# A list scheduler's table of costs and ranks: shorter ways for transfers, a steeper rank for the preparation of later pairs, a lower one for splitting the second weights

## The chip, the core and the metric

The kernel runs on one core of a Trainium2 chip. Its engines are TensorE (PE; its weight loads are listed as PEld), VectorE (DVE), ScalarE (ACT), GpSimd (POOL) and SyncE (SP), which issues nearly all transfers. The metric is device time in microseconds (us), lower is better, given as a median of several runs. One further run was recorded by the profiler; its rows are what is read below.

## The reference, cut to what matters

Three layers follow one another. The first is a recurrence over 768 time steps, for 4 x 8 heads with a 40 x 40 state each:

```python
for t in range(S):                      # S = 768
    y[:, :, t] = einsum('bhd,bhde->bhe', rt, state)
    Sa = einsum('bhde,bhe->bhd', state, at)
    state = state * wt[:, :, None, :] - einsum('bhd,bhe->bhde', Sa, bt)
    state = state + einsum('bhd,bhe->bhde', vt, kt)
x = y.transpose(0, 2, 1, 3).reshape(3072, 320)
x = maximum(maximum(x @ w1, x @ w2), x @ w3) @ w_out      # 320 -> 768 -> 320
x = ((x @ w_a) * (x @ w_b)) @ w_out2                      # 320 -> 1536 -> 320
```

The weights arrive as 64-bit numbers and are split in the kernel into a high and a low part.

## The kernel before, in words

The 768 steps are cut into 24 chunks of 32 steps, and two chunks make a pair (12 pairs, numbered 0 to 11). Inside a chunk the recurrence becomes a small triangular system, so that most of it is matrix work.

**Preparation of a pair** (`prep`, lines 355 to 487, and `solve`, 489 to 544) does not need the state. It loads the pair's inputs, forms running products of the decay (L395, L399 on VectorE), multiplies (L403, L413, L415), forms the products of keys (L446 or L428 on TensorE, L453 or L434 on VectorE), and sends them through DRAM to another layout (L460 writes BD, L466 reads BU). `solve` inverts the triangular blocks by many small steps: a product (L500 on GpSimd, or L501 on VectorE, as the scheduler picks) and a sum (L502 on VectorE). Its results go through DRAM again by two routes: TXp to TD (L472) to TT (L476), and TC to ED (L481) to NB (L484).

**The chain** (`chain`, from line 547) carries the state from chunk to chunk: L617 (it needs ZL), L631 (it needs TT), L644 (it needs NB), L664 (the new state), with copies on ScalarE and sums on VectorE (L672) between them, and at the side the output: L690, L702, L720. The first chunk of a pair is the first to need that pair's TT and NB. A pair's output goes through DRAM (L733 to L740) to the second layer.

**The second layer** (`moe_a`, L828 and L853 to L857 on TensorE) takes 192 matmuls for each pair, and can begin once the pair's output is there and its weights are split (`weights_a`, L760 to L785). **The third layer** (`moe_b`, L982, L990 to L992) begins when all chunks are done; its own weights are split before that by `stage_b` (18 pieces: L920 loads one, L750 to L753 and L922 to L924 split it, L927 and L928 write it to DRAM as WD), and `weights_b` (L934 to L938) fetches them from there.

**What sets the order.** Nothing of this order is written by hand. Each operation is given to a list scheduler (`Plan`) with an engine (or several to choose from), a duration, its reads and writes and a rank `pri`, where a lower one goes first. Ahead of the run the rank is lowered by 0.04 for each microsecond of the longest way from the operation to the end. The scheduler then walks through a modelled time and places whatever can start first; within 0.05 us the better rank wins. Each engine executes in the order so found, and SP issues its transfers in that order too: an instruction that waits holds up all behind it on its engine. A transfer is modelled as 1.2 us from the readiness of its inputs to its issue (`pre`), 0.4 us or more of SP, and a way `lat` until it has landed. The scheduler also inserts fillers (L276: a 128 x 128 matmul of a constant into a free bank, of no use to the result) where its model of TensorE's clock shows too little work.

Of the kernel before, what the change touches and what calls it, by code (L numbers as in the profile page):

```python
# [28 lines left out]
DMIN = 0.4  # L29
# [19 lines left out]
class Plan:  # L49
# [8 lines left out]
    def op(self, eng, dur, fn, r=(), w=(), ps=(), fin=(), pri=0.0, lat=None, after=(), pre=0.0, cls=0, alt=(), act=1.0, bias=None):  # L58

        i = len(self.ops)  # L60
        deps = set(after)
        for k in r:
            if k in self.lw:
                deps.add(self.lw[k])
        for k in w:
            if k in self.lw:
                deps.add(self.lw[k])
            deps.update(self.rd.get(k, ()))
        for k in r:
            self.rd.setdefault(k, []).append(i)  # L70
        for k in w:
            self.lw[k] = i
            self.rd[k] = []
        deps.discard(i)
        ways = {eng: (dur, fn, 0.0)}
        ways.update({e: (d, f, bias if bias is not None else 0.0 if pri < BIASP else BIAS) for e, d, f in alt})
        self.ops.append(dict(i=i, ways=ways, bias=bias, deps=deps, ps=tuple(ps), fin=tuple(fin), pri=pri, lat=lat, pre=pre, cls=cls, act=act))
        return i
# [159 lines left out]
def body(nc, tc, ia, out_ap):  # L238
    from contextlib import ExitStack

    V, A, G, T, SP = nc.vector, nc.scalar, nc.gpsimd, nc.tensor, nc.sync
    es = ExitStack()
    P = Plan(8)
    op = P.op
    npair = NP

    def dv(n, ps=False):
        return 0.15 + n * 0.00105 if ps else 0.12 + n * 0.0014

    def ac(n):  # L250
        return 0.17 + n * 0.0009
# [2 lines left out]
        return 0.4 + n * 0.0023  # L254

    def dma(fn, nbytes, r=(), w=(), pri=0.0, pre=1.2):
        return op("SP", max(DMIN, nbytes / 300e3), fn, r=r, w=w, pri=pri, lat=2.0 + nbytes / 200e3, pre=pre)

    def adma(fn, nbytes, r=(), w=(), pri=0.0, after=()):

# [93 lines left out]

    def prep(p):
        b, kb_ = p % NPB, p % 2
        pr = -0.5 + 0.6 * p
        P_, K_, Z_ = Pp[b], KT[kb_], ZL[b]
        parts = [(0, 1), (1, 2)] if p < NSPL else [(0, 2)]

# [23 lines left out]
        for cc in range(2):  # L384
# [8 lines left out]
            else:  # L393
# [8 lines left out]
               r=[("R", cc, 0), ("R", cc, 1), "d1"], w=rc, pri=pr)  # L402
# [4 lines left out]
            for src, k, n in ((Rp[:, cc, :, 0:32], rc, 1), (P_[:, cc, :, 1:33], pc, 0)):  # L407
                op("ACT", 0.61, lambda w_, cc=cc, src=src, n=n: A.activation(
                    Rp[:, cc, :, 0:32], src, AF.Square, accum_out=gd[:, 4 * p + 2 * cc + n:4 * p + 2 * cc + n + 1]),
                   r=k, w=rc + ["gd"], pri=pr + 0.5)  # L410
            for g in range(2):
# [3 lines left out]
                   r=pc, w=[("Za", b, g, cc)], pri=pr, alt=[("DVE", dv(512), lambda w_, cc=cc, g=g, r0=r0: V.tensor_tensor(  # L415
                       Z_[r0:r0 + 64, cc, g], Z_[r0:r0 + 64, cc, g], P_[r0:r0 + 64, cc, :, 0:32], ALU.mult))])
            pn = ("a", "kb", p, cc)
            za = [("Za", b, g, cc) for g in range(2)]
            if p >= KG:
# [12 lines left out]
                for n in range(4):  # L432
# [5 lines left out]
                       r=[pn, "con"], w=[("Zk", b, g, cc)], fin=[pn] if n == 3 else (), pri=pr)  # L438
# [12 lines left out]
            for g in range(2 if p < KG else 0):  # L451
# [4 lines left out]
                   r=[pn, "con"], w=[("Zk", b, g, cc)], fin=[pn] if g else (), pri=pr)  # L456
# [30 lines left out]
                16e3, r=[("ED", b, h) for h in range(2)], w=[("NB", p % 2, j)], pri=pr)  # L487

    def solve(p):
        pr = -0.5 + 0.6 * p  # L490
        cnt = [0]

        def mm(out_v, tmpshape, a, bb, rk, wk):
            i = cnt[0] % 2
            cnt[0] += 1
            n = int(np.prod(tmpshape))
            names = "abcd"[:len(tmpshape)]
            kw = {k: v for k, v in zip(names[1:], tmpshape[1:])}
            tv = TP[i][:, 0:n].rearrange("p (" + " ".join(names) + ") -> p " + " ".join(names), **kw)
            op("POOL", 0.35 + n * 0.0026, lambda w_: G.tensor_tensor(tv, a, bb, ALU.mult), r=rk, w=[("TP", i)], pri=pr,  # L500
               alt=[("DVE", dv(n), lambda w_: V.tensor_tensor(tv, a, bb, ALU.mult))])  # L501
            op("DVE", dv(n, True), lambda w_: V.tensor_reduce(out_v, tv, AX.X, ALU.add), r=[("TP", i)], w=wk, pri=pr)  # L502

        def diag(tile, off, blk, cnt_, rows, cols, rs=32, cs=1):
            base = tile[:, 0:1, 0:1]
            a = base.copy() if False else base
            return bass.AP(tensor=a.tensor, offset=a.offset + off, ap=[list(a.ap[0]), [blk, cnt_], [rs, rows], [cs, cols]])

        bu = [("BU", 0), ("BU", 1)]
        for t in range(1, 8):  # L510
            a = diag(TX, 0, 264, 2, t, t)
            u = diag(BU, t, 264, 2, 1, t, 0, 32)
            u = bass.AP(tensor=u.tensor, offset=u.offset, ap=[list(u.ap[0]), [264, 2], [0, t], [32, t]])
            o = diag(TX, t, 264, 2, t, 1)
            o = bass.AP(tensor=o.tensor, offset=o.offset, ap=[list(o.ap[0]), [264, 2], [32, t]])
            mm(o, (2, t, t), a, u, bu + ["TX"], ["TX"])

        def prod(dst, d_off, d_rs, L, l_off, l_rs, R, r_off, r_rs, nr, nt, nj, rk, wk):
            tl = 512 // (nt * nj)
            for c0 in range(0, nr, tl):  # L520
                k = min(tl, nr - c0)
                lb, rb, db = L[:, 0:1, 0:1], R[:, 0:1, 0:1], dst[:, 0:1, 0:1]
                a = bass.AP(tensor=lb.tensor, offset=lb.offset + l_off + c0 * l_rs, ap=[list(lb.ap[0]), [l_rs, k], [0, nt], [1, nj]])
                u = bass.AP(tensor=rb.tensor, offset=rb.offset + r_off, ap=[list(rb.ap[0]), [0, k], [1, nt], [r_rs, nj]])
                o = bass.AP(tensor=db.tensor, offset=db.offset + d_off + c0 * d_rs, ap=[list(db.ap[0]), [d_rs, k], [1, nt]])
                mm(o, (k, nt, nj), a, u, rk, wk)


        prod(TW, 0, 8, TX, 0, 32, BU, 8, 32, 8, 8, 8, bu + ["TX"], ["TW"])
        prod(TX, 8, 32, TW, 0, 8, TX, 264, 32, 8, 8, 8, ["TX", "TW"], ["TX"])  # L530

        op("ACT", 0.3, lambda w_: A.activation(BU[64:128, 0:8, 16:32], BU[0:64, 8:16, 16:32], AF.Copy), r=bu, w=[("BB", 0)], pri=pr)
        for h in range(2):
            op("ACT", 0.35, lambda w_, h=h: A.activation(TU[64 * h:64 * h + 64], TX[64:128, :, 0:16], AF.Copy), r=["TX"], w=[("TU", h)], pri=pr)
        k = bu + [("BB", 0), ("TU", 0), ("TU", 1)]
        prod(TC, 0, 16, BU, 16, 32, TU, 0, 16, 8, 8, 8, k, ["TC"])
        prod(TC, 8, 16, BU, 16, 32, TU, 8, 16, 8, 8, 16, k, ["TC"])
# [208 lines left out]
    def convert(raw, ca, m, kr, ka, pri, w=()):  # L746

        hi, lo = (lambda: raw()[:, :, 1]), (lambda: raw()[:, :, 0])
        a = lambda: ca()[:, 0:m]
        op("DVE", 0.12 + m * 0.0012, lambda w_: V.tensor_scalar(a().bitcast(U32), hi(), 3, 0x3FFFFFFF, ALU.logical_shift_left, ALU.bitwise_and), r=[kr], w=[ka, *w], pri=pri)  # L750
        op("DVE", dv(m), lambda w_: V.scalar_tensor_tensor(hi(), hi(), 0xC0000000, a().bitcast(U32), ALU.bitwise_and, ALU.bitwise_or), r=[ka], w=[kr], pri=pri)
        op("DVE", 0.12 + m * 0.0012, lambda w_: V.tensor_scalar(a().bitcast(U32), hi(), 0xFF800000, None, ALU.bitwise_and), r=[kr], w=[ka], pri=pri)
        op("DVE", dv(m), lambda w_: V.scalar_tensor_tensor(lo().bitcast(F32), lo(), 2.0 ** -52, a(), ALU.mult, ALU.mult), r=[ka], w=[kr], pri=pri)  # L753
# [157 lines left out]
    def stage_b():  # L911

        wk, ck = [("wraw", 0), ("wraw", 1)], [("wca", 0), ("wca", 1)]
        r = wrw[:, 0:960].bitcast(U32).rearrange("p (m k) -> p m k", k=2)
        h, a = wrw[:, 960:1440], wcw[:, 0:480]
        for ff in range(LV):
            for q in range(2):
                pr = 3.0
                cs = slice(480 * q, 480 * q + 480)
                dma(lambda w_, ff=ff, cs=cs: SP.dma_start(r, ia["wpb"][ff][:, cs].bitcast(U32).rearrange("p (m k) -> p m k", k=2)), 492e3, w=wk + ["sr", "sw"], pri=pr)  # L920
                convert(lambda: r, lambda: a, 480, "sr", "sa", pr, w=ck)
                i = op("ACT", ac(480), lambda w_: A.activation(h.bitcast(F32R), r[:, :, 1].bitcast(F32), AF.Copy), r=["sr"], w=["sh"], pri=pr)  # L922
                sub = lambda E: (lambda w_: E.tensor_tensor(a, r[:, :, 1].bitcast(F32), h, ALU.subtract))
                add = lambda E: (lambda w_: E.tensor_tensor(a.bitcast(F32R), a, r[:, :, 0].bitcast(F32), ALU.add))  # L924
                op("POOL", po(480), sub(G), r=["sr", "sh"], w=["sa"], pri=pr, alt=[("DVE", dv(480), sub(V))])
                op("POOL", po(480), add(G), r=["sr"], w=["sa"], pri=pr, alt=[("DVE", dv(480), add(V))])
                op("ACT", 0.3, lambda w_, ff=ff, cs=cs: A.dma_start(WD[ff, 0, :, cs], h), r=["sh"], w=[("WD", ff, q, 0), "sw"], pri=pr, lat=3.0, after=[i])  # L927
                dma(lambda w_, ff=ff, cs=cs: SP.dma_start(WD[ff, 1, :, cs], a), 246e3, r=["sa"], w=[("WD", ff, q, 1)] + ck, pri=pr)  # L928
# [334 lines left out]
```

## Time and profile before

| | us |
|---|---|
| runs (median of 3) | 1087.15, 1092.65, 1097.81 (1092.65) |
| the profiled execution's own time | 1090.93 |
| its span, from first to last instruction | 1088.7 |
| first matmul of the third layer (L982) | at 689.4 |
| last output product of the chain (L720) | at 640.38 |

The span falls into a start (0 to 140 us, with hardly any second layer yet), a middle (140 to 640, chain, preparation and second layer interleaved), the rest of the second layer (640 to 690), and the third layer (690 to the end). In the rows below, a matmul of float32 data such as L276 or L617 leaves two records for each instruction, so that a count of 494 stands for 247 instructions; a float32r matmul (L828, L982) leaves one. A busy time counts pipelined matmuls with their whole length; the distance between the starts of two of them is what they cost in time.

### The profile page before, as it was taken

How to read it: one execution, taken by the hardware profiler on the slowest of the kernel's cores; microseconds unless marked ns; L12 is line 12 of the kernel's file. 1: busy time of each engine (PE TensorE's matmuls, PEld its weight loads, DVE VectorE, ACT ScalarE, POOL GpSimd, SP SyncE). 2: the span in 40 equal slices, each digit the busy share in tenths (PEclk: the TensorE clock that was granted, in tenths of full speed). 3: DMA queues.
4: the chain of work that ended last, by engine and by line, in shares of the span. 5: the costliest groups of instructions: out<-in, count | busy, mean ns of one | idle time of the engine just before them, and what ended most of it. 6: DMA issues, size and time to landing. Idle time of an engine off the chain costs nothing.

```text
span 1088.7 us, 34319 instructions
## 1 busy us (share of the span) xinstructions
PE 1034.9 (95%) x14868; PEld 936.6 (86%) x14868; DVE 654.0 (60%) x1091; ACT 480.7 (44%) x1115; POOL 230.1 (21%) x198
## 2 busy tenths in 40 slices
PE   8999789999899998999899999999999999999997
PEld 7878778988798888898889899988888888888886
DVE  7896698968797875989587633475223232332222
ACT  6246546555647373847375532343222232222221
POOL 4441365533423222323320200011000000000000
PEclk9998899899999989999899999999999999999999
DMA  8846875656666847577655547742002000000000
GB/s 272 199 96 161 173 158 126 157 140 167 158 167 153 190 117 189 136 168 166 150 135 149 136 122 204 200 104 62 10 1 54 1 25 1 2 25 1 25 1 27
DMA packets 173437, 123.10 MB, mean 113 GB/s; under 512 B 122464, under 2 KB 147168, under 8 KB 172320
## 3 DMA queue, kind: packets, MB, share of 16 engines
q1 hardware_dynamic: 170688, 116.41, 43.4%
q10 hardware_dynamic: 2592, 4.42, 1.2%
q8 instruction: 119, 1.95, 0.8%
q14 instruction: 38, 0.31, 0.1%
HBM read 93.07 MB, written 27.72 MB: 111 GB/s over the span
## 4 chain that ended last, share of the span: by engine, by line
PE 70%; DVE 12%; DMA 8%; issue 4%; SPq 3%; ACT 1%; POOL 1%; DVEq 0%; POOLq 0%; ACTq 0%
PE bank L982 24%; PE bank L828 11%; PE bank L992 4%; PE bank L990 4%; PE bank L991 4%; PE bank L276 3%; DMA NB<-ED 2%; PE bank L664 2%; PE bank L720 2%; PE bank L644 2%; PE bank L702 2%; PE bank L853 2%; PE bank L854 1%; PE bank L617 1%; PE bank L855 1%
## 5 line engine op out<-in xcount | busy, mean ns | idle before, releaser
L1000 DVE TENSOR_TENSOR bas<-bank,bas 128x512 f32<-128x512 f32 x72 | 49.7, 691 | 188.8 <-PE bank L982 179.8
L982 PE MATMUL bank<-bxhi,bw 128*128 128x512 f32 x576 | 156.3, 393 | 0.0
L982 PEld LDWEIGHTS bank<-bxhi,bw 128*128 128x128 f32 x576 | 106.2, 188 | 20.8
L999 ACT ACTIVATE bas<-bank 128x512 f32<-128x512 f32 x72 | 43.0, 598 | 148.2 <-PE bank L982 144.2
L1002 ACT ACTIVATE bgh<-bas 128x512 fp32r<-128x512 f32 x72 | 45.5, 633 | 125.5 <-DVE bas L1000 125.5
L828 PE MATMUL bank<-xhi,whi 128*128 128x256 f32 x432 | 95.5, 303 | 0.0
L843 DVE TENSOR_TENSOR hm<-bank,hm 128x512 f32<-128x512 f32 x72 | 49.5, 688 | 67.0 <-PE bank L828 66.1
L982 PE MATMUL bank<-bxlo,bw 128*128 128x512 f32 x288 | 89.8, 393 | 0.0
L992 PE MATMUL bank<-bo,bgl 128*128 128x320 f32 x288 | 89.0, 309 | 0.4 <-DVE bgl L1003 0.4
L990 PE MATMUL bank<-bo,bgh 128*128 128x320 f32 x288 | 89.0, 309 | 0.0
L991 PE MATMUL bank<-bo,bgh 128*128 128x320 f32 x288 | 88.9, 309 | 0.0
L828 PE MATMUL bank<-xlo,whi 128*128 128x256 f32 x432 | 88.5, 287 | 0.0
L828 PE MATMUL bank<-xhi,wlo 128*128 128x256 f32 x432 | 88.2, 286 | 0.0
L413 POOL TENSOR_TENSOR ZL<-ZL,Pp 64x512 f32<-64x512 f32 x44 | 58.7, 1334 | 85.4 <-DVE Pp L395 75.0
L1003 DVE TENSOR_TENSOR bgl<-bas,bgh 128x512 fp32r<-128x512 f32 x72 | 49.8, 691 | 43.0 <-ACT bgh L1002 42.8
L276 PE MATMUL bank<-con 128*128 128x128 f32 x494 | 69.2, 293 | 4.0 <-DMA con<-in_con_dram 2.8
L828 PEld LDWEIGHTS bank<-xhi,whi 128*128 128x128 f32 x432 | 67.6, 194 | 2.6
L276 PEld LDWEIGHTS bank<-con 128*128 128x128 f32 x494 | 62.9, 203 | 7.6 <-ACT bank L344 2.8
L828 PEld LDWEIGHTS bank<-xlo,whi 128*128 128x128 f32 x432 | 68.6, 195 | 0.0
L828 PEld LDWEIGHTS bank<-xhi,wlo 128*128 128x128 f32 x432 | 68.4, 195 | 0.0
L982 PEld LDWEIGHTS bank<-bxlo,bw 128*128 128x128 f32 x288 | 54.1, 188 | 12.2
L828 PE MATMUL bank<-xt,wt 128*128 128x256 f32 x216 | 62.0, 287 | 0.0
(181 smaller groups left out, 2446.0 us busy)
## 6 DMA issues: line engine op xcount, KB each, us to landing
wraw<-in_wpb_dram SPq DMA_DIRECT2D x18, 480.0 KB
KT<-in_kb_dram SPq DMA_DIRECT2D x20, 384.0 KB
Pp<-in_wf_dram SPq DMA_DIRECT2D x10, 528.0 KB
Rp<-in_wr_dram SPq DMA_DIRECT2D x10, 528.0 KB
wraw<-in_wpa_dram SPq DMA_DIRECT2D x12, 384.0 KB
bw<-WD SPq DMA_DIRECT2D x9, 512.0 KB
WD<-wraw ACTq DMA_DIRECT2D x18, 240.0 KB
WD<-wca SPq DMA_DIRECT2D x18, 240.0 KB
```

The lines of the kernel that those rows point to most:

```text
L276: P.keep = lambda b: T.matmul(bank[b][:, 0:128], ident, ident, start=True, stop=True)
L413: op("POOL", po(512), lambda w_, cc=cc, g=g, r0=r0: G.tensor_tensor(Z_[r0:r0 + 64, cc, g], Z_[r0:r0 + 64, cc, g], P_[r0:r0 + 64, cc, :, 0: ...
L828: T.matmul(ps, w, x, start=(i == 0), stop=(i == 7))
L843: op("DVE", dv(512, True), lambda w_, pn=pn: V.tensor_tensor(f(hm), bank[w_[pn]], f(hm), ALU.max), r=[pn], w=["hm"], fin=[pn], pri=ep)
L982: T.matmul(ps, w, x, start=(k == 0), stop=(k == 7))
L990: T.matmul(o, gh[:, c], oh, start=ff == 0, stop=False)
L991: T.matmul(o, gh[:, c], ol, start=False, stop=False)
L992: T.matmul(o, gl[:, c], oh, start=False, stop=ff == 11)
L999: op("ACT", ac(512), lambda w_, j=j, pa=pa: A.activation(tb["as", j], bank[w_[pa]], AF.Copy), r=[pa], w=[("bas", j)], fin=[pa], pri=ep)
L1000: op("DVE", dv(512, True), lambda w_, j=j, pb=pb: V.tensor_tensor(tb["as", j], bank[w_[pb]], tb["as", j], ALU.mult), r=[pb], w=[("bas", j) ...
L1002: op("ACT", ac(512), lambda w_, j=j, k=k: A.activation(tb["gh", k], tb["as", j], AF.Copy), r=[("bas", j)], w=[("gh", k)], pri=ep)
L1003: op("DVE", dv(512), lambda w_, j=j, k=k: V.tensor_tensor(tb["gl", k], tb["as", j], tb["gh", k], ALU.subtract), r=[("bas", j), ("gh", k)], ...
```

## The change

Three numbers of the scheduler's tables change, and no operation is added or removed. The way of a transfer issued by SP becomes 1.4 us plus 4 us per MB in place of 2.0 plus 5. The rank of `prep(p)` and `solve(p)`, which was -0.5 + 0.6 p, becomes -0.5 + p. The rank of `stage_b`, which was 3, becomes 4.

```diff
     def dma(fn, nbytes, r=(), w=(), pri=0.0, pre=1.2):
-        return op("SP", max(DMIN, nbytes / 300e3), fn, r=r, w=w, pri=pri, lat=2.0 + nbytes / 200e3, pre=pre)
+        return op("SP", max(DMIN, nbytes / 300e3), fn, r=r, w=w, pri=pri, lat=1.4 + nbytes / 250e3, pre=pre)
...
     def prep(p):
...
-        pr = -0.5 + 0.6 * p
+        pr = 1.0 + p - 1.5
...
     def solve(p):
-        pr = -0.5 + 0.6 * p
+        pr = 1.0 + p - 1.5
...
-                pr = 3.0
+                pr = 4.0
```

As nearly every transfer is counted shorter, the longest ways and with them all ranks move too, and the order of every engine comes out differently.

TensorE, around L631 of chunk 4 (the first chunk of pair 2; TT_141 is its TT). Before:

```order
L446 MATMUL bank_64<-ZL_126,KT_125 64x32 x32
L276 MATMUL bank_67<-con 128x128 x11
L631 MATMUL bank_67<-Zs,TT_141 32x40 x32
L276 MATMUL bank_63<-con 128x128 x9
L446 MATMUL bank_63<-ZL_126,KT_125 64x32 x32
L828 MATMUL bank_68<-xhi,whi 128x256 x2
```

Now:

```order
L276 MATMUL bank_67<-con 128x128 x6
L631 MATMUL bank_67<-Zs,TT_141 32x40 x32
L828 MATMUL bank_68<-xhi,whi 128x256 x2
L828 MATMUL bank_68<-xhi,wlo 128x256 x2
L828 MATMUL bank_68<-xlo,whi 128x256 x2
```

Twenty fillers around this product have become six, the key products of a later pair (L446) have moved away from it, and second-layer matmuls follow it at once.

SP, between the write of TC (L481) and the read of NB (L484) of pair 3 (ED_77 and NB_145). Before:

```order
L476 DMA TT_139<-TD_74 32x16x32 x4
L738 DMA xf<-XD_80 128x2x256
L481 DMA ED_77<-TC 64x128 x2
L863 DMA X2D_83<-x2s 128x512
L460 DMA BD_72<-ZL_127 32x16x32 x2
L740 DMA xf<-XD_80 64x256 x2
L460 DMA BD_72<-ZL_127 32x16x32
L375 DMA Rp<-in_wr_dram 128x1056
L484 DMA NB_145<-ED_77 16x16x16 x4
```

Now:

```order
L476 DMA TT_139<-TD_74 32x16x32 x4
L466 DMA BU<-BD_72 64x512
L466 DMA BU<-BD_72 64x496
L481 DMA ED_77<-TC 64x128 x2
L484 DMA NB_145<-ED_77 16x16x16 x4
L928 DMA WD<-wca 128x480
L920 DMA wraw<-in_wpb_dram 128x960
```

Seven issues stood between the write and the read, and now none does; the next pair's BU reads, which came later, stand ahead of both.

## Rows read from the trace of the kernel before

**Rows 1.** The page's head: span, busy time and share of each engine.
```profile
span 1088.7 us, 34319 instructions
PE 1034.9 (95%) x14868; PEld 936.6 (86%) x14868; DVE 654.0 (60%) x1091; ACT 480.7 (44%) x1115; POOL 230.1 (21%) x198
```

**Rows 2.** Windows by stage: length, busy of each engine, PEclk, DMA share, GB/s.
```profile
0.00:140.00 140.00, 126.66 (x2383) 109.95 (x2384) 107.46 (x194) 72.93 (x191) 53.90 (x50) 0.95 0.72 178
140.00:640.00 500.00, 466.02 (x10007) 434.59 (x10007) 395.40 (x657) 288.41 (x718) 168.56 (x142) 0.96 0.63 152
640.00:690.00 50.00, 50.00 (x469) 49.58 (x469) 16.82 (x28) 11.45 (x21) 0.73 (x1) 1.00 0.75 210
690.00:1089.00 399.00, 392.18 (x2015) 342.49 (x2013) 134.31 (x214) 107.87 (x187) 6.87 (x6) 0.99 0.11 30
```

**Rows 3.** Group of the fillers: busy us, mean ns, idle before.
```profile
L276 PE MATMUL bank<-con 128*128 128x128 f32 x494 | 69.2, 293 | 4.0 <-DMA con<-in_con_dram 2.8 <-DVE XY L724 1.1
```

**Rows 4.** Timeline of PE, 482 to 484: start, length, work; then around 640.
```profile
482.24 0.28 PE L856 MATMUL bank<-hhi,woh 128*128 128x256 f32 x1
482.36 0.28 PE L857 MATMUL bank<-hlo,woh 128*128 128x256 f32 x1
482.48 1.50 PE L276 MATMUL bank<-con 128*128 128x128 f32 x12
483.74 0.48 PE L828 MATMUL bank<-xhi,whi 128*128 128x256 f32 x2
...
640.38 1.42 PE L720 MATMUL bank<-YL,YR 128*40 128x32 f32 x64
```

**Rows 5.** Waits of the span: engine, line, releaser; us, times, longest.
```profile
PE bank L644 <- DMA NB<-ED: 13.6, 9, 3.2
PEld bank L631 <- DMA TT<-TD: 6.9, 10, 2.3
PEld bank L644 <- DMA NB<-ED: 6.7, 6, 2.5
PE bank L631 <- DMA TT<-TD: 5.9, 11, 2.2
```

**Rows 6.** Timeline of SP, 209 to 220: start, length of issue.
```profile
209.31 3.58 SPq L481 DMA_DIRECT2D ED<-TC  x2
...
218.57 1.91 SPq L484 DMA_DIRECT2D NB<-ED  x4
```

**Rows 7.** Chain of waits around 220 and 376: start, us, what; one issue of NB and its landing.
```profile
220.03 3.14 DMA NB<-ED
376.86 4.63 DMA NB<-ED
```

**Rows 8.** One tile, NB: issue durations min/median/max ns, first and last start.
```profile
L484 SPq DMA_DIRECT2D NB<-ED x48: 303/446/628, 63.6 to 616.4; - x48
```

**Rows 9.** Groups of VectorE by form: busy us, mean ns.
```profile
L843 DVE TENSOR_TENSOR hm<-bank,hm 128x512 f32<-128x512 f32 x72 | 49.5, 688 | 67.0 <-PE bank L828 66.1 <-ACT hm L841 0.2
L399 DVE TENSOR_TENSOR_SCAN Rp<-Rp,d 128x528 f32<-128x528 f32 x24 | 35.0, 1458 | 0.5 <-DMA Rp<-in_wr_dram 0.3
L395 DVE TENSOR_TENSOR_SCAN Pp<-Pp,d 128x528 f32<-128x528 f32 x24 | 30.2, 1256 | 3.7 <-DMA TXp<-in_eye_dram 1.9 <-DMA Pp<-in_wf_dram 1.7
```

**Rows 10.** Windows of 20 us: length, busy PE, PEld, DVE, ACT, POOL, PEclk, DMA, GB/s.
```profile
360.00:380.00 20.00, 18.49 (x205) 17.75 (x203) 16.53 (x25) 5.24 (x10) 6.58 (x6) 1.00 0.81 197
380.00:400.00 20.00, 18.38 (x512) 16.63 (x514) 12.75 (x29) 12.56 (x32) 7.68 (x8) 0.83 0.37 83
```

**Rows 11.** One tile, BU: products of solve, durations min/median/max ns.
```profile
L501 DVE TENSOR_TENSOR TP<-BU,TU x19: 1014/1041/2099, 53.4 to 564.4; 128x512 f32<-128x512 f32 x19
L500 POOL TENSOR_TENSOR TP<-BU,TU x17: 1524/1693/3561, 52.6 to 604.4; 128x512 f32<-128x512 f32 x17
```

**Rows 12.** One tile, bw: first transfer's issue and the first L982.
```profile
L982 PE MATMUL bank<-bxhi,bw x576: 387/394/398, 689.4 to 1075.9; 128*128 128x512 f32 x192
L934 SPq DMA_DIRECT2D bw<-WD x9: 366/594/604, 648.2 to 682.2; - x9
```

## The prediction

> **What bounds the kernel now.** First read the head and the windows by stage [rows 1, 2]. TensorE is busy 95% of the span, and the four stages differ. From 690 us on it is never without work for long, nothing else is near its limit, and those 399 us hold only work that the change leaves as it is. From 640 to 690 it is busy throughout with what is left of the second layer. So whatever the change does, it does before 640, where TensorE is busy 593 of 640 us and VectorE 503 of 640. There, read who waits for whom [rows 5]: TensorE waits at L644 for NB and at L631 for TT. These are the two products by which a pair's preparation enters the chain. TensorE's two parts together stand still 20.3 us for NB and 12.8 us for TT. The chain itself is not what is short: between the first products of a pair and its L644 stand second-layer matmuls and fillers, and it is the preparation, VectorE's and GpSimd's many small steps and four transfers in a row, that comes last.
>
> Then the fillers [rows 3]. 494 records are 247 instructions. In the timeline [rows 4] six of them (12 records) occupy TensorE from 482.48 to 483.74, so one costs 0.21 us at the full clock, and all of them some 52 us. Together with the waits and the stretches at half clock (below) this is TensorE's time that holds no useful work, and only this can change.
>
> **The change part by part.** No operation appears or goes. What moves is read from the two orders, what it costs from the rows.
>
> *Fillers.* The order now has 217 of them, 30 fewer: 30 x 0.21 = 6.3 us less. Before L617 of chunk 5 there are 170 in place of 211, and at that place 152 second-layer matmuls have been done in place of 96. So the saving early in the kernel is real work in a filler's place and not an empty place only. Later some comes back: from chunk 12 to 19 the new order adds 27 fillers, the old one 12, since with the second layer further ahead nothing of it is ready (at L644 of chunk 12 exactly 960 matmuls, all five pairs that can be, are done). Bounds: 6.3 us of gain where nothing waits instead, 0 where the data come no earlier and each filler's time becomes a wait. I take the gain, because the useful matmuls that moved in show that the place is not empty.
>
> *Shorter ways.* For NB (16 KB) the scheduler now counts 1.46 us in place of 2.08, for ED 1.53 in place of 2.16, for BD, BU, TD and TT some 1.92 in place of 2.65. With `pre` and the issue this makes for NB 3.06 us from ready to landed, and it was 3.68. The trace has 3.14 us from one issue to the landing, and 4.63 in a busier place [rows 7]. So the new number is a little under the lower row, the old one between the two. What follows is two things of opposite sign.
>
> First, TensorE's instructions may be placed too early. ED and NB follow each other, so the plan can ask for NB 0.62 + 0.63 = 1.25 us sooner in each of the pairs 2 to 11: 12.5 us of waits at most. How much of that the order shows: I added up VectorE's work between the last sum of `solve` (L502 into TC) and the second L672 of the chunk that needs it, by the means of VectorE's groups (the costliest are in [rows 9]). Over pairs 3 to 11 it is 123 us before and 120 now, so the cover of the two transfers shrinks by 0.3 us a pair only. I take 3 us of loss.
>
> Second, SP issues closer. Between the write of TC (L481) and the read of NB (L484) 67 other issues stood in the 12 pairs, now 40. In pair 3 they cost much: ED was issued from 209.31 to 212.89, and NB only at 218.57 [rows 6], though a way of 3.14 us would have ended by about 216. At the median of 0.446 us [rows 8], 27 fewer issues are 12 us of SP's time. But SP must now wait for ED at the head of its queue, with the second weights' transfers and the next chunk's loads behind it, so the most is not to be had. Bounds 0 to 12 us of gain. I take 0, as only the pairs that gate the chain count, and leave the rest to a rival.
>
> *The two ranks.* The steeper slope puts preparation behind: by chunk 6, VectorE has done 195 us of work where it had done 189, with five more us of the second layer in it, and behind the last chunk 513 us in place of 520, because 22 more products of `solve` go to GpSimd (93 in place of 71). A large one takes 1.69 us there and 1.04 on VectorE [rows 11]. Seven large ones more are 4.6 us of `solve`, 0.4 us a pair, and the cover above of some 13 us a pair holds that: 0, and some 5 us if that cover is gone. The lower rank of the second weights costs nothing: its 18th piece is now written ahead of the ninth pair's second layer output (X2D8) on SP, and was written behind it. Nothing near the end waits for it, since bw is not fetched before 648 us [rows 12].
>
> *The handover.* When the last L720 is placed, 328 second-layer matmuls are left in place of 368. At 0.12 us apart [rows 4] that is 39 us, in place of 44, to cover the fetch of the first weights. Issued at 648.2, for a first L982 at 689.4 [rows 12], the fetch has some 41 us. Five less leave 36, still many times a way of 4.63 us. The cost is 0, and what would be late next is the weights of the ninth of the twelve blocks, 44 us later (399 us hold 72 blocks of 5.5 us [rows 2]).
>
> **Sum.** -6.3 + 3 = -3.3 us on a profiled execution of 1090.93 us (1088.7 of span and 2.2 around it), so 1087.6. The median of the runs is 1.7 us above the profiled one, so **1089** against 1092.65. About 1%, 11 us, is what can be told from no change here.
>
> **A page against the row.** For a transfer the trace shows 3.14 and 4.63 us from issue to landing [rows 7]. The Trainium skill, DMA: Bandwidth & Descriptors, section on the anatomy of one DMA (it is on GpSimd's path, these transfers are SP's), puts the fixed part at about 2.0 us, most of it the confirmation of the last write. By that rule the old 2.0 is right, the new 1.4 is 0.6 us too short for every transfer, and the time would be that of the first rival; after its issue of some 0.45 us the row leaves 2.7 us, which agrees with the rule.
>
> **Rivals.**
>
> *The optimism is paid in waits (slower).* The new plan asks for NB 1.25 us too early in pairs 2 to 11, and TensorE, which executes in order, stands still with second-layer matmuls queued behind L644: 12.5 us. Waits also cost clock: behind the wait for NB around 381 the granted clock over 20 us is 0.83 [rows 10], which at the lower of its two levels, 1.2 GHz against 2.4, means 6.8 us of half speed and 3.4 us lost. Three more such stretches make 10 us. Sum: -6.3 + 12.5 + 10 = +16, that is **1109**. It decides from the point where the wait per pair grows by more than 0.6 us, beyond which the fillers' saving is spent. For it: the waits for NB and TT are there already [rows 5], and the new count is under every row. Against it: the 0.3 us that the orders show.
>
> *The closer queue wins (faster).* Half of the 12 us of SP shows up as NB landing earlier where the chain waits, and two of the half-clock stretches go: -6.3 - 6 - 6.8 = -19, with the 3 us loss -16, so **1077**. For it: pair 3, where the gap was longest. Against it: other pairs had fewer issues between, and an SP that waits for ED holds up others.
>
> *GpSimd and VectorE get in each other's way (no change).* The same product takes VectorE 1.04 us at the median and 2.10 at most, GpSimd 1.69 and 3.56 [rows 11], so some run at half speed. With 22 more products on GpSimd, at 0.5 us more for each and half of it uncovered, 5.5 us come on top: **1095**. The Trainium skill, GPSIMD Engine Reference, section on key points, says that GpSimd shares its memory interfaces with VectorE and contends with VectorE instructions of two inputs in SBUF; the longest durations fit that, but no row here separates it.
>
> *The change does not do what it says* is excluded for the orders, as they differ nearly everywhere; for the second weights it holds, since their splitting ends no later. It changes no number.
>
> **Chances.** Forecast 0.45, waits 0.30, closer queue 0.20, contention 0.05. Faster by over 1%: 0.20. Within 1%: 0.45 + 0.05 = 0.50. Slower by over 1%: 0.30. The range from 1074 to 1110 takes in both outer cases, with 3 us below the faster one and little above the slower one. What it leaves out is more waits with more half-clock stretches than I counted. The forecast's own range, by its bounds, is 1082 to 1099.
>
> **What would show it.** Records of L276 should be about 434. The waits of L644 for NB and L631 for TT together should stay near 33 us if I am right, reach 45 or more in the slower rival, and be near 25 in the faster one. The last L720 should come at 640 to 643, since 25 of the fillers saved (5.3 us) and 40 second-layer matmuls more (4.8 us) lie ahead of it, and the first L982 at about 686, with 399 us behind it as before. The low windows of the clock before 640 should be about as many. I am wrong if the third layer's stretch changes, or if the start, up to L617 of chunk 5, comes no earlier though it holds 41 fillers less.

## The result, and the profile after

The changed kernel takes 1081.67 us (median of 20 runs, 1072.21 to 1091.96), the kernel before 1092.64 us on the same chip (20 runs, 1084.8 to 1097.81). The ratio is 0.9895 [0.9876, 0.9915]: 11 us or 1.0% faster. 1089 was forecast. The profiled execution took 1077.52 us, 13.4 less than that of before. A second profile of the same changed kernel, of a later run (`e11_all` below), has a span of 1083.8 in place of 1075.7 us. So a difference of some 8 us between two single traces is no evidence here; the ratios are.

The page's head, and the four stages as windows with the columns of [rows 2]:

```profile
span 1075.7 us, 34217 instructions
PE 1026.0 (95%) x14808; PEld 926.8 (86%) x14808; DVE 644.6 (60%) x1070; ACT 481.1 (45%) x1118; POOL 243.7 (23%) x216
```

```profile
0.00:140.00 140.00, 127.35 (x2430) 110.15 (x2431) 108.18 (x197) 79.36 (x208) 53.82 (x55) 0.96 0.74 183
140.00:640.00 500.00, 469.12 (x10055) 436.98 (x10054) 389.05 (x644) 284.32 (x707) 179.08 (x149) 0.96 0.61 151
640.00:690.00 50.00, 50.00 (x374) 47.92 (x372) 17.61 (x30) 13.69 (x24) 0.73 (x1) 1.00 0.81 241
690.00:1076.00 386.00, 379.55 (x1956) 331.76 (x1954) 129.81 (x203) 103.76 (x180) 10.10 (x11) 0.99 0.09 26
```

TensorE's share is the same 95%. The profile's summary hardly shows the gain; three places in TensorE's timeline do (start, length, work):

```profile
165.24 0.80 PE L617 MATMUL bank<-ZR,ZL 128*32 128x40 f32 x64
633.91 1.42 PE L720 MATMUL bank<-YL,YR 128*40 128x32 f32 x64
675.02 1.17 PE L982 MATMUL bank<-bxhi,bw 128*128 128x512 f32 x4
```

The first row is the L617 of chunk 5, which before came at 174.10:

```profile
174.10 0.80 PE L617 MATMUL bank<-ZR,ZL 128*32 128x40 f32 x64
```

The last L720 comes 6.5 us and the first L982 14.4 us earlier than in [rows 4, 12]. From there to the end it is 400.7 us, before 399.3: the third layer gave nothing. At the L644 of chunk 6 the trace stands at 219.50 (before 222.37), with 368 second-layer matmuls done in place of 280. 88 matmuls at 0.12 us and 2.9 us of time are 13.5 us. **In this trace nearly the whole gain exists before 220 us.** In the second profile the gain is smaller, and in the same place: this L644 stands at 226.58, 4.2 us later than before, but with the same 368 matmuls done, which makes it 6.4 us ahead, and the first L982 comes 6.3 us earlier.

Before 220 us, these are the windows of 20 us for the second layer's L828 alone and for the fillers L276 alone (length, busy us and records of that line, PEclk, DMA share, GB/s). Of before, L828 and then L276:

```profile
120.00:140.00 20.00, 3.03 (x23) 0.86 0.62 135
140.00:160.00 20.00, 5.37 (x43) 0.99 0.82 185
...
140.00:160.00 20.00, 5.00 (x40) 0.99 0.82 185
```

Of after, the same:

```profile
120.00:140.00 20.00, 5.46 (x42) 0.84 0.81 166
140.00:160.00 20.00, 9.35 (x72) 1.00 0.72 173
...
140.00:160.00 20.00, 1.50 (x12) 1.00 0.72 173
```

From 140 to 160 us 40 filler records became 12, and 43 records of L828 became 72, at nearly the same granted clock (0.99 and 1.00). The timeline of TensorE in that stretch shows it in order (the bracket is idle time and what ended it). Before:

```profile
149.27 2.72 PE L276 MATMUL bank<-con 128*128 128x128 f32 x22
151.92 0.27 PE L631 MATMUL bank<-Zs,TT 32*32 32x40 f32 x6
153.02 0.76 PE L631 MATMUL bank<-Zs,TT 32*32 32x40 f32 x58 [0.83 <-DMA TT<-TD]
153.71 2.27 PE L276 MATMUL bank<-con 128*128 128x128 f32 x18
158.93 3.02 PE L446 MATMUL bank<-ZL,KT 40*64 40x32 f32 x64 [2.95 <-DVE KT L403]
```

After:

```profile
142.67 1.50 PE L276 MATMUL bank<-con 128*128 128x128 f32 x12
144.10 0.36 PE L631 MATMUL bank<-Zs,TT 32*32 32x40 f32 x6
144.71 0.76 PE L631 MATMUL bank<-Zs,TT 32*32 32x40 f32 x58 [0.25 <-DMA TT<-TD]
...
153.46 0.39 PE L854 MATMUL bank<-hlo,woh 128*128 128x256 f32 x1 [1.69 <-POOL hlo L845]
```

The same product L631 of chunk 4 stands between 40 filler records before and behind 12 after, and comes 8 us earlier. Before, a wait of 2.95 us for KT, the preparation of a later pair, stood behind it and 18 filler records, with everything else of TensorE queued behind that; it is gone. A shorter one, of 1.69 us for the second layer's own hlo, has come.

Fillers and waits over the span (groups as in [rows 3], waits as in [rows 5]):

```profile
L276 PE MATMUL bank<-con 128*128 128x128 f32 x434 | 64.3, 300 | 3.4 <-ACT bank L344 2.7 <-issue 0.7
```

```profile
PEld bank L631 <- DMA TT<-TD: 13.0, 15, 3.9
PE bank L631 <- DMA TT<-TD: 12.7, 13, 3.7
PE bank L644 <- DMA NB<-ED: 4.7, 7, 2.2
PEld bank L644 <- DMA NB<-ED: 3.3, 6, 0.9
```

The four waits are 33.7 us together, before 33.1; the second profile has 37.4. But they moved: NB went from 20.3 to 8.0 and TT from 12.8 to 25.7. These sums count most of the idle time twice, since TensorE's matmul part (PE) and its weight-load part (PEld) stand still at the same moments (at L631 and L644 24.5 of PE's 24.6 us of idle time are PEld's too); of PE alone the waits for NB and TT are 17.4 us, before 19.5. SP's queue for pair 3 (start, length of issue), and the landing in the chain of waits (start, us), show the closer queue:

```profile
215.05 1.24 SPq L481 DMA_DIRECT2D ED<-TC  x2
217.65 1.78 SPq L484 DMA_DIRECT2D NB<-ED  x4
```

```profile
218.98 2.09 DMA NB<-ED
```

ED is issued in 1.24 us in place of 3.58 [rows 6], and the read comes 1.36 us behind it in place of 5.68. NB has landed at 221.07, before at 223.17 [rows 7]. Yet this pair is not where its wait fell: TensorE comes to this L644 earlier, and stands still for NB 3.09 us there in place of 1.63. The wait fell at chunks 8, 12 and 18, from 3.25, 2.19 and 4.34 us to 0.27, 0 and 0, and the closer queue is not shown to be the cause.

### The profile page after: what moved, and what is told of

The parts are those of the page before. It is cut to its first block, busy times and chain, and to the rows that moved or that the text cites. A ratio compares the mean times of both kernels' runs of the same rounds, so it can differ in the third digit from the quotient of the medians.

```text
span 1075.7 us, 34217 instructions
## 1 busy us (share of the span) xinstructions
PE 1026.0 (95%) x14808; PEld 926.8 (86%) x14808; DVE 644.6 (60%) x1070; ACT 481.1 (45%) x1118; POOL 243.7 (23%) x216
## 4 chain that ended last, share of the span: by engine, by line
PE 70%; DMA 11%; DVE 9%; issue 3%; ACT 2%; SPq 2%; POOL 2%; ACTq 0%; DVEq 0%; POOLq 0%
PE bank L982 25%; PE bank L828 12%; PE bank L990 4%; PE bank L992 4%; PE bank L991 4%; PE bank L276 3%; PE bank L664 2%; DMA BU<-BD 2%; PE bank L720 2%; DMA WD<-wraw 2%; PE bank L644 2%; PE bank L702 2%; PE bank L631 1%; DMA TT<-TD 1%; PE bank L593 1%
## 5 line engine op out<-in xcount | busy, mean ns | idle before, releaser
L982 PE MATMUL bank<-bxhi,bw 128*128 128x512 f32 x576 | 156.4, 393 | 0.0
L982 PEld LDWEIGHTS bank<-bxhi,bw 128*128 128x128 f32 x576 | 106.0, 188 | 20.6
L828 PE MATMUL bank<-xhi,whi 128*128 128x256 f32 x432 | 96.4, 305 | 0.0
L982 PE MATMUL bank<-bxlo,bw 128*128 128x512 f32 x288 | 89.7, 393 | 0.0
L828 PE MATMUL bank<-xhi,wlo 128*128 128x256 f32 x432 | 88.5, 287 | 0.0
L828 PE MATMUL bank<-xlo,whi 128*128 128x256 f32 x432 | 88.3, 287 | 0.0
L500 POOL TENSOR_TENSOR TP<-TXp,BU 128x32 f32<-128x32 f32 (+7 forms) x69 | 46.8, 678 | 110.4 <-DMA BU<-BD 59.5
L828 PEld LDWEIGHTS bank<-xhi,whi 128*128 128x128 f32 x432 | 68.2, 196 | 2.8
L828 PEld LDWEIGHTS bank<-xhi,wlo 128*128 128x128 f32 x432 | 68.8, 195 | 0.0
L828 PEld LDWEIGHTS bank<-xlo,whi 128*128 128x128 f32 x432 | 68.7, 195 | 0.0
L276 PE MATMUL bank<-con 128*128 128x128 f32 x434 | 64.3, 300 | 3.4 <-ACT bank L344 2.7
L413 POOL TENSOR_TENSOR ZL<-ZL,Pp 64x512 f32<-64x512 f32 x42 | 54.2, 1290 | 49.6 <-DVE Pp L395 20.8
L982 PEld LDWEIGHTS bank<-bxlo,bw 128*128 128x128 f32 x288 | 54.1, 188 | 12.3
L276 PEld LDWEIGHTS bank<-con 128*128 128x128 f32 x434 | 58.0, 209 | 7.0 <-ACT bank L344 2.7
```

What stands on the lines that cost most here:

```text
L276: P.keep = lambda b: T.matmul(bank[b][:, 0:128], ident, ident, start=True, stop=True)
L413: op("POOL", po(512), lambda w_, cc=cc, g=g, r0=r0: G.tensor_tensor(Z_[r0:r0 + 64, cc, g], Z_[r0:r0 + 64, cc, g], P_[r0:r0 + 64, cc, :, 0: ...
L828: T.matmul(ps, w, x, start=(i == 0), stop=(i == 7))
L982: T.matmul(ps, w, x, start=(k == 0), stop=(k == 7))
```

## The experiments

The change has three edits. **L** is the shorter ways, **P** the steeper rank of preparation, **S** the lower rank of the second weights. My theory after the result was that P makes the gain, in the start; the rivals were the closer queue of L, the 30 fewer fillers, and S. Each ratio is to the kernel before, run on the same chip, with its 95% interval.

**One edit alone.** Kernels `e1_lat` (L), `e2_prep` (P), `e3_stage` (S) have one of these:

```diff
-        return op(..., lat=2.0 + nbytes / 200e3, pre=pre)
+        return op(..., lat=1.4 + nbytes / 250e3, pre=pre)     # L
-        pr = -0.5 + 0.6 * p
+        pr = 1.0 + p - 1.5                                    # P, in prep and solve
-                pr = 3.0
+                pr = 4.0                                      # S
```

> Only the shorter ways, ranks as before. Its order has 287 fillers, 40 more than before (247), and by L617 of chunk 6 128 second-layer matmuls where before had 176. Theory A (time follows the fillers and the waits that the trace shows, at 0.21 us for a filler): +8 us or more, about 1.01 of before. Theory B (the shorter ways are what made the whole change faster, since SP issues closer: 49 issues between the writes of TC and the reads of NB in place of 67): faster, 0.99. The slower rival of the prediction (optimism paid in waits): the waits of L644 and L631 for NB and TT rise from 33 to 45 us, +16 us, 1.015.

Measured: 1108.1 us, 1.0125 [1.0069, 1.0180]. L alone costs 1.2%.

> Only the steeper rank of prep and solve. 284 fillers, 37 more than before, but by L617 of chunk 6 197 in place of 212. Theory A: +8 us, 1.007. Theory C (the steeper rank alone gives the gain, by earlier second-layer work at the start): 0.99. Waits for NB and TT near 33 us in both.

Measured: 1084.8 us, 0.9903 [0.9870, 0.9936]. P alone makes as much as the whole change, within the intervals, with 37 fillers more. Its waits for NB and TT are 21.2 us, not near 33.

> Only the lower rank of the second weights' splitting. 255 fillers, 8 more. Theory A: +2 us, no change. Theory D (that rank gives the gain): 0.99.

Measured: 1101.15 us, 1.0043 [1.0010, 1.0077]. S alone gives nothing, and rather costs a little.

The closer queue is thus not the source: L brings it (49 issues between in place of 67) and is slower by itself. P moves issues out of that place too (53 are left). But P and S together, below, are among the fastest kernels with waits for NB of 24.2 and 20.7 us in their two profiles, no less than the 20.3 of before. The waits of L alone are these:

```profile
PEld bank L631 <- DMA TT<-TD: 16.5, 15, 2.6
PE bank L631 <- DMA TT<-TD: 14.4, 13, 2.5
PEld bank L644 <- DMA NB<-ED: 8.9, 9, 3.3
PE bank L644 <- DMA NB<-ED: 7.8, 8, 3.2
```

They are 47.6 us, above the 45 that I had named for the slower rival. But most of the growth is the weight-load part's: PE's own are 22.2 us, and were 19.5, and PE's whole idle time ahead of the first L982 is 47.8 us, and was 47.0. What did grow is the fillers, 287 in place of 247 (40 x 0.21 = 8.4 us), and the second layer fell behind: at the L617 of chunk 12 it has 648 matmuls done, where before had 768 and the whole change 824.

**Two edits together.** `e4_lat_prep` (L and P), `e7_prep_stage` (P and S), `e8_lat_stage` (L and S).

> Shorter ways and steeper rank, the second weights' rank as before. 213 fillers, 34 less than before, and up to L617 of chunk 6 the same counts as the whole change (177 fillers, 176 second-layer matmuls). Theory A: -7 us from the fillers and some more from waits, 0.99, like the whole change. Theory D (second weights' rank): no change, 1.00.

Measured: 1083.48 us, 0.9886 [0.9836, 0.9936].

> Steeper rank and the second weights' lower rank, ways as before. 232 fillers, 15 less than before, 52 less than with the steeper rank alone. If time is fillers at 0.21 us plus waits plus half the low-clock time: 0.98 to 0.985, unless its waits grow against the steeper rank alone (36 us of idle TensorE ahead of the third layer). If the steeper rank's gain has nothing to do with fillers: 0.990, as with the steeper rank alone.

Measured: 1081.45 us, 0.9863 [0.9819, 0.9906].

> Shorter ways and the second weights' lower rank, rank of preparation as before. 279 fillers, 32 more than before, and 128 second-layer matmuls by L617 of chunk 6 where before had 176. Fillers at 0.21 us: +6.7 us, about 1.006 to 1.012. If the two together made the gain of the whole change: 0.99.

Measured: 1099.85 us, 1.0014 [0.9977, 1.0052], below what its fillers gave and without the gain.

Every kernel with P, those below included, is 1.0 to 1.7% faster; every kernel without it is at 1.00 or above. P is worth 1.0% alone, 2.4% beside L (0.9886 / 1.0125) and 1.8% beside S (0.9863 / 1.0043). L costs 1.2% alone and nothing to be seen beside P or S. The edits don't add up: each makes a new order.

**Are the fillers the gain?** `e5_less` is the kernel before, in its own order, with 41 fillers of the start left out; `e6_more` is the changed kernel with 41 of them done twice. Nothing else moves.

```diff
+    def keep(w_, ...):
+        count[0] += 1
+        if 150 < count[0] <= 191: return                 # e5_less
...
+        for _ in range(2 if 129 < count[0] <= 170 else 1):   # e6_more
```

> The kernel before, order untouched, with 41 fillers left out (numbers 151 to 191, between the chain's chunks 2 and 4). Theory A (a filler's 0.21 us is TensorE's time): -8.6 us, 0.992. Theory E (there TensorE waits for the preparation anyway, and a filler only covers the wait): no change, 0.998 to 1.002, the first L617 of chunk 5 where it was (174 us), TensorE's waits up to it longer by some 8 us, and perhaps one more stretch at half clock.

Measured: 1094.41 us, 1.0003 [0.9971, 1.0034].

> The changed kernel, order untouched, with 41 fillers doubled (numbers 130 to 170, between chunks 0 and 5), so that L617 of chunk 5 has as many ahead of it as before (211). Theory A: +8.6 us, which takes back most of the gain, 0.997 of before. Theory E: less than 3 us, 0.991 of before.

Measured: 1078.6 us, 0.9864 [0.9810, 0.9919], no slower than the changed kernel.

Taking away 8.6 us of fillers saved nothing that shows, and adding 8.6 us cost nothing that shows: both intervals exclude 0.8%. The first window of each shows what paid for it (columns as in [rows 2]). `e5_less`:

```profile
0.00:140.00 140.00, 123.92 (x2348) 106.95 (x2350) 110.95 (x197) 74.50 (x194) 50.97 (x51) 0.89 0.74 179
```

`e6_more`:

```profile
0.00:140.00 140.00, 130.81 (x2482) 114.51 (x2483) 108.74 (x193) 77.15 (x204) 51.37 (x55) 0.98 0.74 181
```

The granted clock of the start is 0.89 with fewer fillers, where it was 0.95 [rows 2], and 0.98 with more, where the changed kernel has 0.96. Over the timed runs of `e5_less` its mean over the span fell from 0.9725 to 0.9642. That is 0.0083 x 1090 = 9 us more lost to half clock, beside 8.6 us of fillers saved. Over those of `e6_more` it is 0.982, where the 20 runs of the changed kernel have 0.976: some 6 us given back, beside 8.6 us of fillers added. Theory E had the result right and its main reason wrong: the waits of `e5_less` did not grow (46.8 us of gaps ahead of the first L982, before 47.0), and the half clock, which it gave as a perhaps, took all.

**Where P works.** `e9_early` keeps the steep slope for the first four pairs only, `e10_late` for the later ones only; L and S are in both.

```diff
-        pr = 1.0 + p - 1.5
+        pr = -0.5 + p if p < 4 else 2.5 + 0.6 * (p - 3)     # e9_early
+        pr = -0.5 + 0.6 * p if p < 4 else 1.3 + p - 3       # e10_late
```

> The changed kernel, with the steeper rank only up to pair 3 (from pair 4 on the old slope of 0.6 a pair, going on from 2.5). Theory F (the gain is second-layer work that the steeper rank brings into the start, where the preparation of pairs 2 and 3 sets the pace): as the whole change, 0.985 to 0.992, with 152 second-layer matmuls ahead of L617 of chunk 5. Theory G (the gain is in the middle, from a slope that holds for all pairs): at most half of it, 0.995 or more.

Measured: 1078.21 us, 0.9828 [0.9787, 0.9869].

> The changed kernel, with the old slope up to pair 3 and the steeper one only behind it. Theory F: no gain, about as shorter ways and lower second weights' rank alone, 0.998 to 1.01, with 80 second-layer matmuls ahead of L617 of chunk 5. Theory G: 0.99.

Measured: 1104.87 us, 1.0085 [1.0051, 1.0119].

The slope over the first four pairs gives the whole gain, and the slope behind them adds nothing. In `e9_early` the later pairs keep the rise that the first four gave (their rank is 1.2 above that of before), so this rise may belong to it. The L617 of chunk 5 in the two, as timeline rows:

```profile
169.84 0.80 PE L617 MATMUL bank<-ZR,ZL 128*32 128x40 f32 x64
```

```profile
181.98 1.30 PE L617 MATMUL bank<-ZR,ZL 128*32 128x40 f32 x64
```

The early one reaches it at 169.84 with 152 second-layer matmuls done, as many as the whole change; the late one 12 us later with 80. The sum made above at the L644 of chunk 6 (the time there, and 0.12 us for each second-layer matmul done) separates all kernels alike: each one whose first pairs have the steep rank is 6 to 14 us ahead of before in its trace, and each one without it lies between 1 us ahead and 10 us behind. L alone is 1.2 us behind there and 9.6 at its first L982, so its loss comes later.

**The best of them?** `e11_all` is the whole change once more, `e12_prep_stage` is P and S, on one chip.

> The whole change once more, on the chip of this set: 0.987 to 0.992.

Measured: 1080.94 us, 0.9860 [0.9823, 0.9898].

> Steeper rank and second weights' rank without the shorter ways, beside the whole change on one chip. If the shorter ways add nothing to the other two: equal to the whole change or up to 0.5% faster, 0.983 to 0.99. If they are needed: slower than the whole change by 3 us or more.

Measured: 1077.15 us (1069.80 to 1080.09), 0.9826 [0.9786, 0.9865]. It and `e9_early` lie lowest, but their intervals overlap with that of `e11_all`, and `e7_prep_stage`, the same kernel on another chip, had 0.9863. So the shorter ways aren't needed; that they cost something beside P isn't shown.

**One account for all.** I split the time of the first L982, in the one profile of each, into fillers (0.21 us each), the gaps between TensorE's matmuls ahead of it, the half clock's loss ((1 - mean granted clock) x span), and a rest:

| kernel | first L982 | fillers | gaps | half clock | rest |
|---|---|---|---|---|---|
| before | 689.4 | 51.9 | 47.0 | 27.2 | 563.3 |
| after | 675.0 | 45.6 | 42.5 | 25.8 | 561.1 |
| `e11_all`, the same kernel | 683.2 | 45.6 | 47.7 | 24.9 | 565.0 |
| `e1_lat` | 699.0 | 60.3 | 47.8 | 26.4 | 564.5 |
| `e2_prep` | 684.0 | 59.6 | 36.4 | 21.7 | 566.3 |
| `e5_less` | 686.8 | 43.3 | 46.8 | 35.8 | 560.9 |
| `e6_more` | 677.3 | 54.2 | 38.4 | 18.3 | 566.4 |
| `e10_late` | 703.0 | 56.1 | 54.3 | 32.0 | 560.6 |

The rest is 560 to 566 us in these and the six others: the useful work. What a new order can win is the sum of the three columns, and **no one column alone tells the result**: `e2_prep` has 37 more fillers than before, and is 1% faster.

## Why the prediction was right, and where it failed

The forecast of 1089 lay 7 us above what came, further than the 1077 of the faster rival, whose mechanism (NB landing earlier) did not make the gain. The range from 1074 to 1110 held, but it was wide enough for both rivals. The forecast's own range, 1082 to 1099, was just missed (1081.67), and 1.05% falls into "faster by over 1%", which had 0.20. So the range held in part by luck. The forecast's own range is not the sum of the bounds given, either: those come to 1074 and 1110. The stage held, and so did the mechanism named for the start (real work in a filler's place). Its size didn't, and it was put down to the wrong part of the change.

*The two ranks, "0": this step failed.* I asked only what the slope does to GpSimd's share of `solve`, and left the preparation's place in the start out of it. The runs give P alone -1.0%, beside L -2.4%, and all of it from the slope over the first four pairs. There TensorE has empty time: 211 of the 247 fillers of before stand ahead of the L617 of chunk 5. With the slope, second-layer matmuls stand in TensorE's order where the next pair's key products (L446) stood, and the 56 more of them that I had read off the order (152 in place of 96, 6.7 us at 0.12) run in time that was fillers and waits. I had that number and used it only to support the fillers' term. That P makes the gain is shown by the runs; that it does so in this way is read from the orders and traces.

*Fillers, -6.3: the count right, the price wrong.* 434 records came. But the 41 fillers that went in `e5_less` saved nothing by themselves, and the clock lost as much as they took; the price of 0.21 us holds only where useful work moves in. It is no term beside the second layer's work but the same one seen from the other side. "Bounds 6.3 to 0" had the wrong lower case in mind, a new wait; in `e5_less` it was the clock.

*Shorter ways, +3: right in the sum of the waits, by accident.* NB and TT wait 33.7 us, with 33 forecast. But NB fell from 20.3 to 8.0 and TT rose from 12.8 to 25.7: the wait moved to the other route of the same preparation, which I hadn't put into either rival. That goes with L: in every kernel with L the waits for TT are 21.0 to 34.8 us and those for NB 7.7 to 16.7, in every one without it 8.1 to 16.0 and 13.1 to 24.2. And the sum was a poor sign. It adds PE's and PEld's idle time, which coincide, so that the 12.5 us of the slower rival would have shown about twice; and it is 42.5 us in `e9_early`, which is 1.7% faster, and 35.3 in `e10_late`, which is 0.85% slower. The reading of [rows 7] was wrong too: 3.06 us counts from the readiness of the inputs, 3.14 from the issue. From issue to landing the new table counts 0.4 + 1.46 = 1.86 us and the old one 2.48, and both lie under both rows. By itself L is the slower rival in sign and nearly in size (1.0125, some 14 us; I gave +16). Its place is another, though: not TensorE's idle time, which is 47.8 us against 47.0, but 40 more fillers over a second layer that fell behind. Beside P none of that shows.

*Second weights, 0* holds within what can be told: +0.4% alone, no sign that lasts beside the others. *The handover, 0* and the unchanged third layer hold: 400.7 us behind the first L982 against 399.3. The first L982 was forecast at about 686 and came at 675.0 and 683.2 in two profiles; the last L720, forecast at 640 to 643, came at 633.9 and 642.0. The two profiles differ by 8 us in both. Of the 32 windows of 20 us before 640, 4 in either have a granted clock under 0.9, before 6.

*GpSimd against VectorE* didn't show. The same product as in [rows 11], now 18 times on each:

```profile
L501 DVE TENSOR_TENSOR TP<-BU,TU x18: 1031/1056/2050, 54.8 to 601.0; 128x512 f32<-128x512 f32 x18
L500 POOL TENSOR_TENSOR TP<-BU,TU x18: 1478/1632/2965, 54.6 to 596.9; 128x512 f32<-128x512 f32 x18
```

Median and longest are about as before, though GpSimd does 93 products of `solve` in place of 71, and 29 of this shape in all in place of 22.

*The page against the row.* The NB of pair 3 took 2.09 us from issue to landing, and 1.64 without an issue of 0.45. The Trainium skill, DMA: Bandwidth & Descriptors, section on the anatomy of one DMA, has about 2.0 us fixed, for GpSimd's path; this transfer, which SP issued, went below it, and the 2.7 us of [rows 7] lay 0.7 above, which I had called agreement. By its rule the new count is too short and the kernel slower: with L alone it was, though not by TensorE's idle time; in the whole change it was not.

**Open.** What exactly the preparation was pushed behind in the start wasn't separated. Besides the second layer's own work, the last piece of the first weights is split 7 us earlier (193.8 before, 186.8 after), and an order that moves one of the two alone wasn't run. But the earlier splitting isn't needed for the gain: P alone has that last piece at 195.9, and P and S together have it at 192.9 and 198.4. Nor is it settled how much of the 11 us is in the gaps: the two profiles of the changed kernel have 42.5 and 47.7 us, before had 47.0.

## What to carry to other kernels

In a kernel whose busiest engine is padded with fillers, count the useful work that moves into the padded stretch, not the fillers that go. Look for the gain of a rank where another resource sets the pace and the busy engine has nothing to do, here the first 220 us. And take a bundle of scheduler constants apart before keeping it: of these three one made the gain, one showed none, and one cost 1.2% where it stood alone.

## What the hardware showed that I had not expected

In the start of this kernel TensorE's idle padding and its clock cancel within what can be told. 41 fillers fewer lowered the mean granted clock of the timed runs from 0.9725 to 0.9642, and the time stayed the same (1.0003 [0.9971, 1.0034]); 41 more raised it from 0.976 to 0.982, and the changed kernel's gain stayed too (0.9864 [0.9810, 0.9919]). And two profiles of one kernel with one order differ by 8 us of span, 5 of them in gaps of TensorE, so that a single trace cannot settle a difference of half a per cent.
